# Halo rows of a fused attention and gated-FFN kernel: computed twice, or taken from the neighbouring token column

## The chip, the core and the metric

The kernel runs on one core of one Trainium2 chip. The metric is device time in microseconds (us) of one execution. Five engines matter: TensorE (PE, with its weight loads PEld), VectorE (DVE), ScalarE (ACT), GpSimd (POOL), and SyncE (SP), whose queue issues most of the transfers.

## The reference, cut to what matters

```python
# attention: x (4, 4160, 192), weight_gen (4, 4160, 8 heads, 7 taps)
w = np.exp(weight_gen - np.max(weight_gen, axis=-1, keepdims=True))
w = w / (np.sum(w, axis=-1, keepdims=True) + 1e-09)
x_pad = np.concatenate([np.zeros((B, 6, D)), x], axis=1)
x_unf = x_pad[:, np.arange(S)[:, None] + np.arange(7)[None, :], :]
x = np.einsum('bshk,bskhg->bshg', w, x_unf.reshape(B, S, 7, 8, 24)).reshape(B, S, D)
# gated FFN: w_in (192, 1024), conv_w (3, 1024), w_out (1024, 192)
h = np.maximum(x @ w_in, 0.0)
hp = np.concatenate([zeros(B, 1, 1024), h, zeros(B, 1, 1024)], axis=1)
conv_out = sum(conv_w[k] * hp[:, k:k + S, :] for k in range(3))
out = (h / (1.0 + np.exp(-conv_out))) @ w_out
```

Each output token needs seven tokens of x (itself and the six before it), and h of its own token, of the one before and of the one after.

## The kernel before

The 4 x 4160 tokens are cut into 128 segments of 130 tokens, one to a partition of the attention part; the 32 segments of one batch lie on neighbouring partitions. A **row** is one token of every segment: 128 tokens, 130 apart. Attention for a row works with the 128 tokens on the partitions. Its result is transposed on PE, and from there on a row is 128 **columns** of a matrix whose partitions are channels.

The convolution needs the row before the first and the row after the last, which are tokens of neighbouring segments. The kernel before computes them again: it loads the neighbours' x and weights (`load_x`, `load_w`), runs attention and the first matmul on row -1 and row 130 like on any other, and thus has 132 rows in 33 **blocks** of four (`R = 4`, `NB = 33`). Block 0 holds rows -1 to 2, block 32 rows 127 to 130. Rows outside a batch are zeroed with masks (`edge`, `zero`, `keep`).

Per block:

- **Attention** (`attention`, `head`, `tap`): seven products of x and the softmaxed weights ("taps") into the tiles px (taps 0 to 3) and py (taps 4 to 6). Weights come in **groups**: group 0 serves block 0, group 1 blocks 1 and 2, group 2 blocks 3 and 4. `SMX` names, by group, the engines of the softmax's subtraction and of its normalisation (with the zeroing). In blocks 0 to 2 PE transposes all seven taps and adds them up in a PSUM bank (two banks, tp for channels 0 to 127, ops for the other 64); `PLAN` names the engine of each tap. Later blocks add the taps by transfers.
- **Split** (`split_hi`, `split_lo`): the sum is split in two parts of lower precision, the tiles H1, H2 and L1.
- **Eight units**, one for 128 channels of h each (`unit`): five matmuls of 512 columns into a bank z (`mm1`); on ACT relu into h and the middle term of the convolution back into z (`relu`, `wmid`); on DVE the two side terms (`conv_side`, once per neighbour); on ACT the gate as a tanh (`sig`); on DVE the product into g (`gmul`). There are five banks z (`NZ = 5`), so a unit's first matmul waits for the `gmul` five units earlier.
- **Tiles** (`out_tiles`): for each row 8 pairs of matmuls of 192 columns, g times w_out, into a bank; ACT copies it out (`evac`), SP stores it (`store`). The tiles of a block stand on PE among the units of the block two later, except at the end; the tiles of block 1 stand among the units of block 2. Block j gives the rows whose neighbour after is known, so block 0 gives two rows, the others four.
- **Carry** (`carry`): the last two rows of h are copied to its front for the next block.

Before block 0 can finish, w_in, conv_w and w_out are decoded on ACT and DVE from their raw words (`dec`); `CH` lists the pieces of w_in, `WOE` names the engines for w_out, `FORD` the order of block 0's units.

The order on each engine isn't written out by hand. A list of tasks with estimated durations is put in order by a planner: earliest start first, then the rank `now` (block number plus an offset: `TO` for attention, `FO` for transposes, `WO_` for tiles), then one pass backward and one forward. All instructions are issued in this order, and every engine runs its own in order. Task kind "VK" marks DVE work that the planner keeps apart from POOL work: behind it DVE and POOL each write a one-column tile `tok`, and POOL waits there for DVE.

## Time and profile before

| | |
|---|---|
| three timed runs, median (range) | 707.25 us (706.74 to 707.96) |
| the profiled execution | 706.31 us |
| its span (first to last instruction) | 704.3 us |
| PE busy | 683.6 us, 97% |
| DVE busy | 629.0 us, 89% |
| ACT busy | 554.5 us, 79% |
| POOL busy | 514.9 us, 73% |
| granted TensorE clock | 0.999 |

The span is what the trace shows; the execution's own time has 2.0 us more around it. Busy shares are averages over stages. In rows of the timeline, the first two numbers are start and duration in us, and what stands in brackets is how long the engine had nothing to run before it, and what ended that.

### The profile page before, as it was taken

How to read it: one execution, taken by the hardware profiler on the slowest of the kernel's cores; microseconds unless marked ns; L12 is line 12 of the kernel's file. 1: busy time of each engine (PE TensorE's matmuls, PEld its weight loads, DVE VectorE, ACT ScalarE, POOL GpSimd, SP SyncE). 2: the span in 40 equal slices, each digit the busy share in tenths (PEclk: the TensorE clock that was granted, in tenths of full speed). 3: DMA queues.
4: the chain of work that ended last, by engine and by line, in shares of the span. 5: the costliest groups of instructions: out<-in, count | busy, mean ns of one | idle time of the engine just before them, and what ended most of it. 6: DMA issues, size and time to landing. Idle time of an engine off the chain costs nothing.

```text
span 704.3 us, 10972 instructions
## 1 busy us (share of the span) xinstructions
PE 683.6 (97%) x3749; PEld 623.3 (89%) x3749; DVE 629.0 (89%) x1005; ACT 554.5 (79%) x1079; POOL 514.9 (73%) x422
## 2 busy tenths in 40 slices
PE   1899999999999999999999999999999999999998
PEld 1788999999999999999999999999999999999998
DVE  6999999999999999999899899988898888888881
ACT  3588888887888888878787787888878778888881
POOL 3998987998999888897776878877777788730000
PEclk9999999999999999999999999999999999999999
DMA  7736998999999888797988889788888887781211
GB/s 236 214 92 166 218 205 207 211 226 213 207 223 217 202 199 194 178 207 170 218 190 201 197 163 223 176 213 193 189 188 184 177 184 167 171 194 67 78 44 45
DMA packets 70787, 127.59 MB, mean 181 GB/s; under 512 B 5046, under 2 KB 42573, under 8 KB 70732
## 3 DMA queue, kind: packets, MB, share of 16 engines
q0 software_dynamic: 20160, 58.99, 47.5%
q1 hardware_dynamic: 50090, 67.51, 29.6%
q8 instruction: 29, 0.48, 0.3%
q10 hardware_dynamic: 482, 0.40, 0.2%
q14 instruction: 26, 0.21, 0.1%
HBM read 20.51 MB, written 12.78 MB: 47 GB/s over the span
## 4 chain that ended last, share of the span: by engine, by line
PE 96%; DVE 2%; DMA 1%; POOL 0%; issue 0%; ACT 0%; POOLq 0%
PE ops L424 47%; PE z L378 43%; PE tp L340 4%; PE ops L340 1%; DMA stage<-in_moe_conv_w_dram 1%; PE z L424 1%; DMA stage<-in_moe_w_in_dram 0%; DVE py L292 0%; POOL px L292 0%; POOL py L292 0%; DVE r L257 0%; DVE m L248 0%; DVE w L242 0%; DVE px L292 0%; DVE dps L146 0%
## 5 line engine op out<-in xcount | busy, mean ns | idle before, releaser
L395 DVE SCALAR_TENSOR_TENSOR z<-h,cw,z 128x512 f32<-128x512 f32 (+1 forms) x528 | 377.6, 742 | 21.6 <-ACT z L388 15.7
L424 PE MATMUL ops<-wo,g 128*128 128x192 f32 x2048 | 353.1, 326 | 0.0
L424 PEld LDWEIGHTS ops<-wo,g 128*128 128x128 f32 x2048 | 338.9, 190 | 9.8
L378 PE MATMUL z<-H,wi 128*128 128x512 f32 x1056 | 303.8, 409 | 1.0 <-ACT wi L614 1.0
L292 POOL TENSOR_TENSOR px<-ring,w 128x768 f32<-128x768 f32 (+2 forms) x146 | 230.9, 1698 | 67.2 <-PE tp L340 67.0
L378 PEld LDWEIGHTS z<-H,wi 128*128 128x128 f32 x1056 | 191.1, 188 | 32.8 <-ACT wi L614 1.4
L402 ACT ACTIVATE z<-z 128x512 f32<-128x512 f32 (+1 forms) x264 | 150.7, 571 | 53.4 <-DVE z L395 51.7
L411 DVE SCALAR_TENSOR_TENSOR g<-z,h 128x512 f32<-128x512 f32 (+1 forms) x264 | 177.0, 678 | 12.3 <-ACT z L402 10.3
L388 ACT ACTIVATE z<-h,cw 128x512 f32<-128x512 f32 (+1 forms) x264 | 179.7, 684 | 6.2
L384 ACT ACTIVATE h<-z 128x512 f32<-128x512 f32 x264 | 155.4, 591 | 15.8 <-PE z L378 15.6
L292 POOL TENSOR_TENSOR py<-ring,w 128x768 f32<-128x768 f32 (+2 forms) x108 | 163.3, 1826 | 2.2 <-DMA px<-py 2.2
L378 PE MATMUL z<-L,wi 128*128 128x512 f32 x264 | 103.0, 390 | 0.0
L325 POOL TENSOR_TENSOR px<-px 128x512 f32<-128x512 f32 (+1 forms) x60 | 72.9, 1466 | 5.3 <-DMA px<-px 5.3
L360 ACT ACTIVATE H<-tp 64x256 fp32r<-64x256 f32 (+1 forms) x93 | 42.3, 454 | 22.0 <-PE tp L340 21.7
L378 PEld LDWEIGHTS z<-L,wi 128*128 128x128 f32 x264 | 49.5, 188 | 11.2
L433 ACT ACTIVATE o<-ops 128x192 f32<-128x192 f32 x128 | 42.1, 329 | 19.2 <-PE ops L424 16.7
L318 POOL DMA_DIRECT2D px<-px x30 | 36.7, 1224 | 15.3 <-DMA px<-py 12.9
L315 POOL DMA_DIRECT2D px<-py x30 | 40.4, 1346 | 8.5 <-POOL py L292 8.5
L340 PE MATMUL tp<-ident,px 128*128 128x128 f32 x228 | 38.0, 281 | 2.8 <-POOL px L292 2.0
L340 PEld LDWEIGHTS tp<-ident,px 128*128 128x128 f32 x228 | 30.0, 145 | 8.7 <-POOL px L292 2.5
L364 DVE TENSOR_TENSOR H<-tp,H 64x256 fp32r<-64x256 f32 x60 | 25.4, 423 | 7.7 <-ACT H L360 5.8
L364 DVE TENSOR_TENSOR L<-tp,H 128x512 fp32r<-128x512 f32 x33 | 22.7, 688 | 8.7 <-ACT H L360 8.6
(67 smaller groups left out, 181.4 us busy)
## 6 DMA issues: line engine op xcount, KB each, us to landing
px<-py POOLq DMA_DIRECT2D x30, 1152.0 KB, 9.9
h<-h SPq DMA_DIRECT2D x128, 256.0 KB, 4.4
px<-px POOLq DMA_DIRECT2D x30, 768.0 KB, 6.6
ring<-in_x_dram SPq DMA_DIRECT2D x31, 384.0 KB, 6.7
out_dram<-o SPq DMA_DIRECT2D x31, 384.0 KB, 5.8
w<-in_weight_gen_dram SPq DMA_DIRECT2D x15, 224.0 KB, 6.0
r_out<-in_moe_w_out_dram SPq DMA_DIRECT2D x4, 384.0 KB, 5.6
wi<-scr SPq DMA_DIRECT2D x8, 128.0 KB, 6.2
```

The costliest lines, as they stand in the source:

```text
L292: eng.tensor_tensor(out=dst[:, a:b, :].rearrange("p s (h g) -> p s h g", g=GRP), in0=ring[:, p:p + n, :].rearrange("p s (h g) -> p s h g", ...
L325: nc.gpsimd.tensor_tensor(out=dst.rearrange("p (s d) -> p s d", s=R), in0=a[:, :, lo:hi], in1=b[:, :, lo:hi], op=ALU.add)
L340: nc.tensor.matmul(o, lhsT=a, rhs=ident, is_transpose=True, start=(start and c == 0), stop=(stop and c == len(ops) - 1))
L360: nc.scalar.activation(out=hi, in_=src, func=ACTF.Copy)
L364: nc.vector.tensor_tensor(out=lo, in0=src, in1=hi.bitcast(F32), op=ALU.subtract)
L378: nc.tensor.matmul(out=z, lhsT=w[:, fs], rhs=h_t[j, nm], start=(i == 0), stop=(i == len(terms) - 1))
L384: nc.scalar.activation(out=hrow(f, 2, R), in_=z_t[j, f], func=ACTF.Relu)
L388: nc.scalar.activation(out=z_t[j, f][:, :no * P], in_=hrow(f, cc, no), func=ACTF.Copy, scale=cw[:, NF + f:NF + f + 1])
L395: nc.vector.scalar_tensor_tensor(out=z, in0=hrow(f, cc + d, no), scalar=cw[:, k * NF + f:k * NF + f + 1], in1=z, op0=ALU.mult, op1=ALU.add,)
L402: nc.scalar.activation(out=z, in_=z, func=ACTF.Tanh, scale=0.5)
L411: nc.vector.scalar_tensor_tensor(out=g_of(j, f), in0=z_t[j, f][:, :no * P], scalar=1.0, in1=hrow(f, cc, no), op0=ALU.add, op1=ALU.mult)
L424: nc.tensor.matmul(out=ps[:, 0:D], lhsT=g_of(j, f)[:, i * P:(i + 1) * P], rhs=wo[:, f, :], start=(f == 0), stop=(f == NF - 1),)
```

## The change

The halo rows are no longer computed. Block 0 has three rows (0 to 2), block 32 has three (127 to 129). A row that needs a neighbour's h takes it from the neighbouring column of the same matrix: row 130 of a segment is row 0 of the next, row -1 is row 129 of the one before.

- **Block 0**: x from six tokens back and not seven, no extra weight row, taps of 576 and not 768 elements, three transposes a tap, matmuls of 384 columns. Row 0's convolution is left open: `side_next` puts its middle and following terms in the SBUF tile `zs`, and only row 1 is finished. Row 2 is finished by block 1, as before. `keep0` copies h of row 0 to the tile `hs`, four transfers of two units each.
- **Block 32**: matmuls of 384 columns; row 129's following term comes from `hs`, shifted by one column inside a batch (128x4x31), so that the first side term takes two instructions.
- **Row 0's end**: when block 32's h is there, `left0` adds the missing term from row 129, one column to the left, eight times; `sig0` and `gmul0` work on four units at once; then row 0's tile (`row0`) is computed and stored.
- **Chosen anew**: softmax engines (group 0 "GV" for "VV", group 1 "GG" for "VV", group 3 "VV" for "GG"), the first piece of w_in decoded in SBUF with its clamp and remainder on POOL, the order of block 0's units, the ranks TO, FO, WO_, the assumed arrival times, and `WOE` (of whose letters only the last counts here).

```diff
-SMX = ("VV", "VV", "GG", "GG")
+SMX = ("GV", "GG", "GG", "VV")
-TO = -2.7
-FO = -0.35
-WO_ = 1.62
+TO = -1.55
+FO = -0.4
+WO_ = 1.52
-    ("f", 0, 256, 5.2, "VGP", "G"),
-    ("m", 0, 256, 8.7, "VVP", "G"),
+    ("f", 0, 256, 5.2, "GVS", "G"),
+    ("m", 0, 256, 10.4, "VVP", "G"),
-FORD = (0, 3, 1, 5, 2, 4, 7, 6)
+FORD = (0, 1, 3, 2, 7, 5, 4, 6)
...
+    def fresh(j):
+
+        return (0 if j else 1), (R if j < NB - 1 else R - 1)
...
+        a, b = fresh(j)
         for i, (w, nm) in enumerate(terms):
-            nc.tensor.matmul(out=z, lhsT=w[:, fs], rhs=h_t[j, nm], start=(i == 0), stop=(i == len(terms) - 1))
+            nc.tensor.matmul(out=z[:, a * P:b * P], lhsT=w[:, fs], rhs=h_t[j, nm][:, a * P:b * P], start=(i == 0), stop=(i == len(terms) - 1))
...
+    def side_next(j, f):
         no, cc = geom(j)
+        z = z_t[j, f]
+        if j == 0:
+
+            side(zs[:, f], hrow(f, cc + 1, 1), z[:, 0:P], 2, f)
+            side(z[:, P:2 * P], hrow(f, cc + 2, 1), z[:, P:2 * P], 2, f)
+        elif j == NB - 1:
+
+            n = (no - 1) * P
+            side(z[:, :n], hrow(f, cc + 1, no - 1), z[:, :n], 2, f)
+            zl_ = by_seq(z[:, n:n + P])[:, :, 0:PB - 1]
+            side(zl_, by_seq(hs[:, f])[:, :, 1:PB], zl_, 2, f)
...
+    def left0(f):
+        z = by_seq(zs[:, f])[:, :, 1:PB]
+        side(z, by_seq(h[:, f, R, :])[:, :, 0:PB - 1], z, 0, f)
...
+    def keep0(f0):
+        nc.sync.dma_start(out=hs[:, f0:f0 + CG, :], in_=h[:, f0:f0 + CG, 3, :])
...
         out_tiles(NB - 2)
+        now[0] = NB - 1 + WO_
+        hold0 = {}
+
+        def row0():
+            hold0[0] = mm2(NB, 0)
+        a_ = task("P", 0.03 + NF * 0.326, rd0 + bank[1], row0)
...
         out_tiles(NB - 1)
```

The order on the engines moves with it. Three places matter; in the rows the names are the tiles of the code with a running number, so px_305 and px_286 are block 1's px before and after, and each row ends with partitions x elements and a count.

**POOL, from block 0's py taps to block 1's first taps.** Before:

```order
L895 MEMSET tok2_101 128x1
L292 TENSOR_TENSOR py_218<-ring_98,w_118 128x768
L895 MEMSET tok3_102 128x1
L895 MEMSET tok4_103 128x1
L292 TENSOR_TENSOR px_185<-ring_98,w_118 128x768
L242 TENSOR_TENSOR w_143<-w_143,m_278 128x448
L292 TENSOR_TENSOR px_305<-ring_98,w_135 128x768 x2
```

After, where w_134 is group 1's weights and w_142 group 2's:

```order
L279 TENSOR_TENSOR px_174<-ring_98,w_120 128x576 x2
L227 TENSOR_TENSOR w_134<-w_134,m_187 128x448
L953 MEMSET tok2_101 128x1
L279 TENSOR_TENSOR py_208<-ring_98,w_120 128x576 x2
L245 TENSOR_TENSOR w_134<-w_134,r_188 128x448
L953 MEMSET tok3_102 128x1
L279 TENSOR_TENSOR px_174<-ring_98,w_120 128x576
L227 TENSOR_TENSOR w_142<-w_142,m_241 128x448
L251 TENSOR_TENSOR w_134<-w_134,edge_93 128x168
L279 TENSOR_TENSOR px_286<-ring_98,w_134 128x768 x3
```

Group 1's subtraction, normalisation and zeroing now stand on POOL among block 0's taps; there are two waits for DVE where there were three, and the two py taps stand behind one of them together.

**PE, from block 0's tiles to the first tile of block 1.** Before (g_403 is block 0's, g_649 block 1's; z_751 to z_794 are the first five units of block 2):

```order
L424 MATMUL ops_709<-wo_96,g_403 128x192 x8
L424 MATMUL ops_728<-wo_96,g_403 128x192 x8
L378 MATMUL z_751<-H1_680,wi_95 128x512 x2
...
L378 MATMUL z_794<-L1_681,wi_95 128x512
L424 MATMUL ops_804<-wo_96,g_649 128x192 x8
```

After (g_366 is block 0's, g_663 block 1's; z_677 to z_702 are the last three units of block 1, z_723 to z_778 the first five of block 2):

```order
L458 MATMUL ops_653<-wo_96,g_366 128x192 x8
...
L372 MATMUL z_677<-H1_456,wi_95 128x512 x2
...
L372 MATMUL z_702<-L1_457,wi_95 128x512
L372 MATMUL z_723<-H1_648,wi_95 128x512 x2
...
L372 MATMUL z_778<-L1_649,wi_95 128x512
L458 MATMUL ops_786<-wo_96,g_663 128x192 x8
```

One tile of block 0 is left there, and it has moved ahead of three units of block 1; nothing but units stands between it and block 1's first tile.

**DVE, the last unit of block 32.** Before (z_6211 and z_6237 are the last two units):

```order
L395 SCALAR_TENSOR_TENSOR z_6237<-h_97,cw_94,z_6237 128x512 x2
L411 SCALAR_TENSOR_TENSOR g_6172<-z_6211,h_97 128x512
L411 SCALAR_TENSOR_TENSOR g_6172<-z_6237,h_97 128x512
```

After (z_6197 and z_6223 are the last two):

```order
L388 SCALAR_TENSOR_TENSOR z_6223<-h_97,cw_94,z_6223 128x384
L388 SCALAR_TENSOR_TENSOR z_6223<-hs_109,cw_94,z_6223 128x4x31
L388 SCALAR_TENSOR_TENSOR z_6223<-h_97,cw_94,z_6223 128x512
L444 SCALAR_TENSOR_TENSOR g_6157<-z_6197,h_97 128x512
L444 SCALAR_TENSOR_TENSOR g_6157<-z_6223,h_97 128x512
L388 SCALAR_TENSOR_TENSOR zs_110<-h_97,cw_94,zs_110 128x4x31 x6
L425 SCALAR_TENSOR_TENSOR zs_110<-zs_110,hs_109 128x512 x2
```

Each unit has three side instructions and not two, and six of the eight `left0` and both `gmul0` come behind the last `gmul`; on PE row 0's tile follows directly on the first of block 32's four.

## Rows read from the trace of the kernel before

**Rows 1.** The page: span, and busy time, share and instructions by engine.

```profile
span 704.3 us, 10972 instructions
PE 683.6 (97%) x3749; PEld 623.3 (89%) x3749; DVE 629.0 (89%) x1005; ACT 554.5 (79%) x1079; POOL 514.9 (73%) x422
```

**Rows 2.** The chain that ended last, first 100 us: start, duration, what.

```profile
28.36 3.23 PE z L378 x13
...
64.18 5.68 PE z L378 x25
69.86 2.60 PE ops L424 x16
```

**Rows 3.** Timeline of PE at the start.

```profile
18.48 1.06 PE L340 MATMUL tp<-ident,px 128*128 128x128 f32 x4
19.34 1.06 PE L340 MATMUL ops<-ident,px 128*64 128x128 f32 x4
...
22.11 0.60 PE L340 MATMUL tp<-ident,py 128*128 128x128 f32 x4
22.54 0.60 PE L340 MATMUL ops<-ident,py 128*64 128x128 f32 x4
...
28.36 0.70 PE L378 MATMUL z<-H,wi 128*128 128x512 f32 x2 [1.01 <-ACT wi L614]
```

**Rows 4.** Timeline of DVE, the first 29 us.

```profile
5.00 0.39 DVE L239 TENSOR_REDUCE m<-w 128x32 f32<-128x224 f32 x1 [1.56 <-DMA w<-in_weight_gen_dram]
...
15.72 0.94 DVE L292 TENSOR_TENSOR px<-ring,w 128x768 f32<-128x768 f32 x1
...
17.99 1.70 DVE L292 TENSOR_TENSOR py<-ring,w 128x768 f32<-128x768 f32 x1
...
28.30 0.42 DVE L619 TENSOR_TENSOR wi<-dps,wi 128x256 fp32r<-128x256 f32 x1
```

**Rows 5.** Timeline of POOL, the first 25 us.

```profile
11.96 1.54 POOL L292 TENSOR_TENSOR px<-ring,w 128x768 f32<-128x768 f32 x1
...
17.34 1.54 POOL L292 TENSOR_TENSOR py<-ring,w 128x768 f32<-128x768 f32 x1
...
22.21 1.55 POOL L292 TENSOR_TENSOR px<-ring,w 128x768 f32<-128x768 f32 x1
23.71 0.97 POOL L242 TENSOR_TENSOR w<-w,m 128x448 f32<-128x448 f32 x1
```

**Rows 6.** DMA issues of the first 3 us, with us from issue to landing.

```profile
ring<-in_x_dram SPq DMA_DIRECT2D x1, 588.0 KB, 7.0
...
w<-in_weight_gen_dram ACTq DMA_DIRECT2D x1, 84.0 KB, 2.5
...
w<-in_weight_gen_dram ACTq DMA_DIRECT2D x1, 3.3 KB, 3.0
```

**Rows 7.** DVE groups by form, 28.6 to 67.5 us: busy us, mean ns.

```profile
L395 DVE SCALAR_TENSOR_TENSOR z<-h,cw,z 128x512 f32<-128x512 f32 x16 | 11.1, 745 | 0.0
L395 DVE SCALAR_TENSOR_TENSOR z<-h,cw,z 128x256 f32<-128x256 f32 x16 | 7.2, 476 | 0.0
...
L411 DVE SCALAR_TENSOR_TENSOR g<-z,h 128x256 f32<-128x256 f32 x8 | 3.3, 409 | 0.0
```

**Rows 8.** Timeline of DVE, the last two gmul of block 1.

```profile
66.11 1.35 DVE L411 SCALAR_TENSOR_TENSOR g<-z,h 128x512 f32<-128x512 f32 x2
```

**Rows 9.** The chain that ended last, its last 20 us.

```profile
685.58 5.20 PE ops L424 x32
690.78 2.60 PE z L424 x16
...
701.22 0.33 ACT o L433
```

**Rows 10.** Timeline of DVE, its last instructions.

```profile
688.42 1.43 DVE L411 SCALAR_TENSOR_TENSOR g<-z,h 128x512 f32<-128x512 f32 x2
```

**Rows 11.** Waits of DVE, 655 to 705 us: total us, times, longest.

```profile
DVE z L395 <- ACT z L388: 2.3, 4, 1.0
```

More of the change, by code (lines that the diff above doesn't have):

```diff
@@ L121 @@
     scr = [const.tile([P, 3, W], I32, name=f"scr{i}") for i in range(2)]
+    hs = const.tile([P, NF, P], F32, name="hs")
+    zs = const.tile([P, NF, P], F32, name="zs")
     EXP_OFF = 2.0 ** -112
@@ L279, in sm_ops, with cols @@
         )
+    def cols(q):
+        return (0 if q else 1), R
     def tap_cut(q, k):
@@ L286, in tap @@
         c = R - tap_cut(q, k)
-        for a, b in ((0, c), (c, R)):
-            if a == b:
+        for a, b in ((0 if q else 1, c), (c, R)):
+            b = min(b, cols(q)[1])
+            if a >= b:
                 continue
@@ L337, in transposes @@
             src = piece(q, i)
-            ops = [(dst[0:D2 if part else P, c * P:(c + 1) * P], src[:, c, part * P:part * D2 + P]) for c in range(R)]
+            ops = [(dst[0:D2 if part else P, c * P:(c + 1) * P], src[:, c, part * P:part * D2 + P])
+                   for c in range(cols(q)[0], R)]
         for c, (o, a) in enumerate(ops):
@@ L430, in evac @@
     def evac(j, i, ps):
-        if i == 0:
+        if j not in o_t:
             o_t[j] = o_p.tile([P, R, D], F32, tag="o", name="o")
@@ L713, in head @@
                     pr = i < 0 and part == 1
-                    f_ = task("P", 0.24 if pr else 0.46, [e_] + (bank[b_] if first else [prev[part]]), fold)
+                    f_ = task("P", 0.24 if pr else 0.46 if q else 0.35, [e_] + (bank[b_] if first else [prev[part]]), fold)
                     prev[part] = f_
@@ L724, in head, with tile_rows @@
                 yf_.append(task("none", 0.0, yend))
-        zl, last_mm, mm_end = [], [None], {}
+        zl, last_mm, mm_end, hk, l0, rd0 = [], [None], {}, {}, [], []
+        def tile_rows(j):
+            return range(0 if j else 1, geom(j)[0])
         def unit(j, f):
@@ L731, in unit @@
             now[0] = j + (FORD.index(f) if j == 0 else f) / NF
+            nr = fresh(j)[1] - fresh(j)[0]
             mm[n] = task(
[L733 removed]
+                "P", 1.135 if nr == R else 0.86, spl_done[j] + w_rdy[f] + zl[-NZ:][:1] * (len(zl) >= NZ),
+                lambda: mm1(j, f), after=[last_mm[0]])
             last_mm[0] = mm_end[j] = mm[n]
[L735 to L739 removed]
+            no = geom(j)[0]
+            m_ = (no if j else 1) * P
+            r_ = task("A", act(nr * P), [mm[n], ca.get(n - NF), hk.get(n - NF)] + ([] if j else [c2]), lambda: relu(j, f))
+            y_ = task("A", act(no * P, 1) + 0.04, [r_, c2], lambda: wmid(j, f))
+            cv_ = task("V", vec(m_) + 0.27 * (nr < R), [y_] + ([hk[f]] if j == NB - 1 else []), lambda: side_next(j, f))
+            cv_ = task("V", vec(m_), [cv_], lambda: side_prev(j, f))
             t_ = task("A", act(m_) + 0.02, [cv_], lambda: sig(j, f))
[L741 removed]
+            dep = [tiles[j - 2, i] for i in tile_rows(j - 2)] if j >= 2 else wo_rdy if j else []
             rd[n] = gm[n] = task("V", vec(m_, 0), [t_] + dep, lambda: gmul(j, f))
+            if j == NB - 1:
+                l0.append(task("VK", vec(P, 0), [r_], lambda: left0(f)))
+                if f % 4 == 3:
+                    a_ = task("A", act(W), l0[-4:], lambda: sig0(f - 3, f + 1))
+                    rd0.append(task("VK", vec(W, 0), [a_], lambda: gmul0(f - 3, f + 1)))
             zl.append(gm[n])
@@ L749, in unit @@
                     ca[k] = c_
+                if j == 0:
+                    c_ = dma(0.2 * CG, [gm[k] for k in ns], lambda: keep0(f0))
+                    for k in ns:
+                        hk[k] = c_
         zfree, last_evac, stored = [], [], []
@@ L754, in out_tiles @@
             d_ = 0.03 + NF * 0.326
-            no = geom(j)[0]
-            for i in range(no):
+            for i in tile_rows(j):
                 now[0] = j + WO_ + i / R
@@ L766, in out_tiles @@
                     after=[tiles.get((j, i - 1))])
[L767 removed]
+                e_ = task("A", act(D) + 0.02, [a_] + (stored[-4:][:1] if i == tile_rows(j)[0] and len(stored) > 3 else []),
                           lambda hold=hold: evac(*hold[0]), begun=last_evac)
@@ L793 @@
         out_tiles(NB - 2)
+        now[0] = NB - 1 + WO_
[3 more added lines that the diff above has]
+        a_ = task("P", 0.03 + NF * 0.326, rd0 + bank[1], row0)
+        e_ = task("A", act(D) + 0.02, [a_] + stored[-4:][:1], lambda: evac(*hold0[0]), begun=last_evac)
+        last_evac[:] = [e_]
+        bank[1] = [e_]
+        stored.append(dma(0.4, [e_], lambda: store(NB, 0, 1)))
         out_tiles(NB - 1)
```

100 lines of the change are left out of this document (45 added, 55 removed).

## The prediction

> **What bounds the kernel now.** I read the page first: PE is busy for 97% of a span of 704.3 us, DVE for 89% [rows 1]. The chain that ended last says the same more sharply. From 28.36 us to the end it runs on PE alone [rows 2]; the last piece is the copy of the last tile at 701.22 [rows 9]. Ahead of 28.36 PE waits for the first sums of taps, for their split and for the decoded w_in, and what is late there is made by POOL and DVE in turn. So the change can gain in three places: less work on PE, an earlier start of PE's unbroken run, and a shorter end. The timelines of DVE and POOL at the start, and of DVE where block 1 ends, say how much of each arrives at the last tile.
>
> **Less work on PE.** 25 matmuls of 512 columns take 5.68 us [rows 2], 0.227 each and 1.135 for a unit of five. No row has a matmul of 384 columns of this kind. In proportion it takes 0.170 and a unit saves 0.28; at worst it costs what 512 columns cost and saves nothing. I take 0.27, near proportion: 2.2 us for the eight units of block 0 and 2.2 for those of block 32, each between 0 and 2.3. Block 0 also has 14 transposes fewer, but they lie ahead of the unbroken run. The tiles stay 130 of 2.60 us; one of block 0's two moves to the end. That is nothing in PE's total, but 2.6 us of cover less at the start and 2.6 us of work more at the end.
>
> **The start on POOL.** Before, the first POOL tap begins at 11.96 and block 0's last tap at 22.21, so it ends at 23.7 [rows 5]. The weights of group 0 need one transfer and not three: the segments' own landed 2.5 us after issue, the last little one 3.0 after its later issue [rows 6], and DVE waited 1.56 us for it until 5.00 [rows 4]. That moves the softmax by about 1.4 us, but x then ends last: its 588 KB took 7.0 us to land [rows 6], and six rows in place of seven make that perhaps half a microsecond less, so x is there at about 9.6. Then come DVE's first tap (0.94 us for four rows [rows 4], 0.7 for three), two small decode steps and the hand-over: POOL's first tap at about 11.1, bounds 10.6 and 12.0. A tap of three rows is 1.54 x 3/4 = 1.16 us. Two taps end at 13.4; group 1's subtraction, moved here from DVE (0.97 us for its like on POOL [rows 5]), at 14.4; exponential, sum and hand-over take 1.2, to 15.6; two py taps to 18.0; the normalisation to 19.0. The third hand-over waits for DVE's decode of conv_w and of the next piece of w_in, 0.8; the last tap ends at 21.0, which is 2.7 us earlier than before.
>
> **From the last tap to the units.** Four transposes take 0.86 us start to start at 18.48 and 0.43 at 22.11 [rows 3]; the granted clock is 0.999 of 2.4 GHz over the execution and doesn't explain the two, so I price by these rates as they stand. PE stands mostly still until 19 us after the change, and 18 transposes of block 0 then follow the last hand-overs: 2.0 us at the fast rate, 3.9 at the slow one, and 1.1 for the split. The first unit starts at 24.1 to 26.0; I take 24.7. Before, the first unit had two of its five matmuls done and a wait of 1.01 us when the run began at 28.36 [rows 3], which is as if it had begun at 27.9. DVE's last step for the second piece of w_in ended at 28.7 [rows 4]; with the split ahead of it by 2.7 us less some idle time it ends at about 26.4, bounds 25.5 and 27.5.
>
> **DVE from there to the end of block 1.** Before, DVE goes from 28.7 to the last gmul of block 1, which ends at 67.4 [rows 8]: 38.7 us, almost without idle time. The list stays the same but for block 0's units. An instruction of 512 columns takes 0.745, of 256 columns 0.476 [rows 7], start to start 0.08 less; the straight line through these gives 0.26 for 128 columns (0.19 for a gmul, from its 0.409). A unit had two sides and a gmul of 256 columns, 1.11 us; it gets three sides and a gmul of 128, 0.97. Eight units save 1.1 us and the narrower splits 0.3, while one side of block 2, 0.66, now stands ahead of the last gmul: 38.0 us. That gmul then ends at 26.4 + 38.0 = 64.4, bounds 62.5 and 66.0.
>
> **What PE does meanwhile.** By PE's own work, block 1's first tile would come at 24.7 + 6.9 (block 0's units) + 12.1 (112 transposes at 0.108) + 9.1 (block 1's units) + 2.6 (a tile) + 5.7 (five units of block 2) = 61.1. But the fifth unit of block 2 needs the bank that the last gmul of block 1 gives back, and the tile needs its g. So that unit starts at 64.5 and the tile at 65.7: PE, which was the bound here, waits about 4.6 us for DVE over the first units of block 2. Before, the tile came at 69.86 [rows 2] and DVE had been ready 1 us ahead of the fifth unit. Shift: **-4.2 us**, between -6 and -2.5.
>
> **From that tile to the last.** PE's work is the same but for 2.2 us less in block 32 and row 0's tile, 2.6 more: **+0.4**. In the blocks between, PE is full and DVE is not; the softmax of group 3, moved to DVE, lies behind the shift and takes its idle time there. The saved rows' transfers and the eight new ones (h to hs) are off the path: block 1 reads h back only after its own units.
>
> **The end.** PE's last unit ends at 685.58, two tiles cover 5.20, and block 32's first tile begins at 690.78 [rows 9]; DVE's last gmul ends at 689.85 [rows 10], 0.9 earlier. After the change PE comes to this point 2.2 us sooner, while DVE has more to do: a unit's following term costs 0.26 for 31 x 4 columns more and 0.13 less for the 384, eight times 0.13, and two of the `left0` stand ahead of the last gmul, 0.5: 1.6 us. Together that is 3.7 against 0.9 of room and against the idle time that DVE has there, of which 2.3 us is waiting for ACT's middle term [rows 11]. Row 0's tile begins 2.6 after block 32's first and needs six `left0` and one `gmul0` behind the last gmul, 6 x 0.26 + 0.65 = 2.2. If no idle time is given up, PE waits 3.7 - 0.9 + 2.2 - 2.6 = 2.4 us; if all is, nothing. I take **+0.6**.
>
> **Sum.** -4.2 + 0.4 + 0.6 = -3.2 us. Against the profiled execution, 706.31 with 2.0 us around its span, that is 703.1. The median of the timed runs, 707.25, lies 0.94 above this execution, so the forecast for a median is 704.0. A change under 0.2%, 1.4 us, can't be told from none here.
>
> **Rivals.** (A) *DVE doesn't hold PE back.* If DVE gets through its list faster, with earlier inputs from PE, the tile comes when PE's own work allows, at 61.1: -8.8 + 0.4 + 0.6 = -7.8, 699.4. For it: PE is the only bound that the chain shows. Against it: DVE's 38.7 us for block 0 and 1 had no idle time to give, and half of A is the most that I'd expect. (B) *The end eats it.* DVE gives up no idle time and PE waits the 2.4 us: 705.8. For it: DVE's waits there are for ACT, which has a fixed order too. (C) *The hand-overs cost more than the narrower taps save: slower.* Place: DVE's instructions between the three `tok` waits. DVE's py tap took 1.70 us where its px tap took 0.94 [rows 4]; POOL's tap ran from 17.34 to 18.88 [rows 5], so it waited 0.8 for POOL. With group 1's softmax on POOL, three DVE steps (its py tap and two steps for conv_w) can each meet a POOL instruction of about 1 us, and POOL then waits at the next tok for what DVE did late. From a last tap at 24.2 on, 3.2 later than I have it, nothing is left; three full collisions and conv_w landing 1.5 late make 4.5, 708.5. The Trainium skill's page "SBUF — State Buffer", section "SBUF: two separate sides", says that DVE and GpSimd share a port pair as an exclusive lock, held for a whole instruction; the 0.8 us in this trace agrees. (D) *384 columns cost as much as 512*: the change doesn't do what it says on PE; block 32 saves nothing, +2.2: 706.2.
>
> **How the numbers follow.** Forecast 0.62, A 0.13, B 0.12, C 0.08, D 0.05. The time is the forecast's, 704.0; its own range by the bounds of DVE's front and of the end is 701.5 to 706. The range to hold 8 in 10 reaches down past A to 698.9 and up past B and D to 706.4. Faster by over 0.2% means below 705.8: the forecast but for 0.02 of it, A, and half of B, 0.79. Within 0.2%: the other half of B, D, and 0.03 of the forecast and of C, 0.14. Slower: the rest of C, 0.07.
>
> **What the profile after would show.** Right: a first unit on PE at 24 to 26 us with matmuls of 384 columns at about 0.175 start to start; DVE without idle time from 26 to 64; PE idle before z in the first units of block 2, released by DVE's gmul; block 1's first tile at about 65.7; a period of PE per block as before; at the end, waits of PE under 1 us around row 0's tile. Wrong: that tile at 61 with no wait (A); PE waiting over 2 us for zs (B); POOL's last tap of block 0 behind 23.7 (C); the units of block 32 still 1.135 apart (D).

## The result, and the profile after

The changed kernel takes **717.53 us**, median of four runs (714.57 to 719.27), against 707.41 for the kernel before (706.74 to 707.96): a ratio of 1.0139, with a 95% interval of 1.0104 to 1.0174. It is slower by 1.4%, outside the range of the prediction and on its other side. The profiled execution is the one of 717.59 us.

The page, answering to [rows 1]:

```profile
span 715.9 us, 10928 instructions
PE 685.7 (96%) x3735; PEld 624.3 (87%) x3735; DVE 630.9 (88%) x1026; ACT 562.0 (79%) x1081; POOL 514.2 (72%) x424
```

The span grew by 11.6 us while no engine has notably more to do: PE is 2.1 us busier with 14 matmuls fewer. The chain that ended last gives the first hint. Before, 96% of it ran on PE; now it does for 74%, with 8% on transfers and 8% on POOL. So somewhere PE now waits for a chain of POOL work and transfers. The timeline of PE shows where (start, duration, what; in brackets the idle time before it and what ended it):

```profile
26.90 0.96 PE L372 MATMUL z<-H,wi 128*128 128x384 f32 x4
...
27.88 0.85 PE L372 MATMUL z<-H,wi 128*128 128x384 f32 x4
...
28.75 0.60 PE L328 MATMUL tp<-ident,px 128*128 128x128 f32 x4
...
64.82 1.19 PE L372 MATMUL z<-H,wi 128*128 128x512 f32 x4 [1.15 <-DVE g L444]
...
68.69 2.76 PE L458 MATMUL ops<-wo,g 128*128 128x192 f32 x16
72.72 1.20 PE L372 MATMUL z<-H,wi 128*128 128x512 f32 x4 [1.27 <-DVE g L444]
...
90.92 2.76 PE L458 MATMUL ops<-wo,g 128*128 128x192 f32 x16
...
285.14 0.72 PE L372 MATMUL z<-H,wi 128*128 128x512 f32 x2 [2.11 <-ACT h L379]
...
286.09 4.25 PE L458 MATMUL ops<-wo,g 128*128 128x192 f32 x16
...
448.64 0.41 PE L328 MATMUL tp<-ident,px 128*128 128x128 f32 x2 [3.02 <-DVE L L353]
448.88 4.45 PE L458 MATMUL ops<-wo,g 128*128 128x192 f32 x16
...
702.11 2.76 PE L458 MATMUL ops<-wo,zs 128*128 128x192 f32 x16
```

In the timeline of before, the first tiles of blocks 1 and 2 are:

```profile
69.70 2.76 PE L424 MATMUL ops<-wo,g 128*128 128x192 f32 x16
...
89.91 2.76 PE L424 MATMUL ops<-wo,g 128*128 128x192 f32 x16
```

The reader is to see three things. Block 1's first tile stands at 68.69, where it stood at 69.70 (69.86 in the chain, [rows 2]). The start has thus gained 1.0 us, not 4.2. Of that nothing is left at block 2's first tile, 90.92 now and 89.91 before. In the middle of the program, where PE never stood still before, it stands still for 2.11 and 3.02 us, and the tile behind each stop takes 4.25 and 4.45 us instead of 2.76; a third, shorter stop, 0.83 us at 409.37, lies between them. And the end is as it should be: row 0's tile at 702.11 has no wait at all, where 0.6 was forecast. The last matmul ends at 712.7, 11.5 later than before.

The steady part can be told by one row of a table by stretch (window, its length, PE's busy time with its instructions, granted clock, share and rate of transfers), first before, then after:

```profile
125.00:660.00 535.00, 535.00 (x2909) 1.00 0.83 190
```

```profile
125.00:660.00 535.00, 529.04 (x2855) 0.99 0.83 188
...
286.00:288.00 2.00, 2.00 (x7) 0.50 0.01 0
...
450.00:453.00 3.00, 3.00 (x11) 0.51 0.33 99
```

Before, PE has no idle time in these 535 us. After, it has 5.96, and behind each of the two stops the granted clock is at 0.50 and 0.51, the lower level of 1.2 GHz, so that 1.49 and 1.69 us more go to the two tiles. Between the tiles just before and after the stops PE loses 4.06 (256 to 300 us) and 5.9 us (341 to 468 us, the short stop included) against the kernel before. The account: +1.0 at block 2's first tile, +10.0 in the stops, some +0.4 in the rest: 11.4 of the 11.5.

**What PE waits for.** From block 3 on the taps are added by transfers, and POOL's queue issues them. A block's first sum (`fold1`, px<-py, 1152 KB) is issued after its last py tap; the second (`fold2`, px<-px) needs the first to have landed, and waits on POOL's queue with everything of POOL behind it; then `fold3` adds the last two parts on POOL. Each block goes once around this ring of POOL work and a transfer. Here is POOL before and after, at about the same time:

```profile
341.16 1.55 POOL L292 TENSOR_TENSOR px<-ring,w 128x768 f32<-128x768 f32 x1 [4.00 <-PE tp L340]
342.95 1.22 POOL L318 DMA_DIRECT2D px<-px  x1 [0.25 <-issue]
343.73 3.52 POOL L292 TENSOR_TENSOR px<-ring,w 128x768 f32<-128x768 f32 x2
...
353.17 1.73 POOL L315 DMA_DIRECT2D px<-py  x1
```

```profile
343.61 1.22 POOL L305 DMA_DIRECT2D px<-px  x1 [3.93 <-DMA px<-py]
346.27 4.54 POOL L279 TENSOR_TENSOR px<-ring,w 128x768 f32<-128x768 f32 x3 [1.44 <-PE tp L328]
...
357.20 1.24 POOL L302 DMA_DIRECT2D px<-py  x1
...
370.50 1.22 POOL L305 DMA_DIRECT2D px<-px  x1 [3.55 <-DMA px<-py]
```

Before, one px tap of the next block stands ahead of `fold2` (L318). POOL waits 4.00 us with that tap for PE, which still reads the tile that the tap will overwrite, and when it is done the transfer has landed too: the slack of the ring is used up in a wait for PE, and PE is the bound. After, `fold2` (L305, at 343.61) stands ahead of all the taps, and POOL waits for the landing first. From block 6 on this is so in four blocks; in the others the new order shifts other work. The waits of POOL over the whole execution say the same (total us, times, longest):

```profile
POOL px L292 <- PE tp L340: 67.0, 19, 4.9
POOL px L318 <- DMA px<-py: 12.9, 7, 5.0
```

```profile
POOL px L305 <- DMA px<-py: 47.8, 16, 6.0
POOL px L279 <- PE tp L328: 42.3, 12, 4.9
```

Together that is 90.1 us where it was 79.9, and now more for the transfer than for PE. And in the chain of after, ahead of the second stop, transfers stand in place of matmuls (two of four rows):

```profile
357.20 12.77 DMA px<-py
...
378.09 11.18 DMA px<-py
```

For the comparison of runs I use two numbers, worked out from the 27 pairs of issues in POOL's timeline from 100 to 720 us. **A** is the mean time from the issue of a `fold2` to that of the next `fold1`: POOL's part of the ring, work and waits. **T** is the mean from a `fold1` to its `fold2` where POOL waited for the landing: the transfer's part. Such turns are few (6 before, 14 after, one or two in e10 and e11). On the mean a ring has room as long as A + T lies under PE's 20.24 us a block. Before, A is 7.93 and T 10.56, together 18.5; after, 8.58 and 10.80 (longest 13.3), together 19.4. What the expectations call W is POOL's work alone in its part of the ring, added up from the mean times of taps and sums: 7.31 before, 7.86 after.

**The link to PE.** PE doesn't wait for the sums themselves in these 535 us. What it waits for shows on ACT and POOL, first at the first stop (the timelines of after):

```profile
281.52 0.58 ACT L230 ACTIVATE w<-w 128x448 f32<-128x448 f32 x1 [4.61 <-POOL w L227]
```

```profile
279.57 2.85 POOL L227 TENSOR_TENSOR w<-w,m 128x448 f32<-128x448 f32 x2
```

A softmax's subtraction (L227) stands on POOL behind a `fold2` that waited 3.40 us for px<-py; ACT's exponential waits for it, and in order behind that stand relu and the middle term of the units, for which PE then waits (`<-ACT h` at 285.14). The second stop comes by the same link, over ACT's gate and DVE's `gmul` and split (`<-DVE L` at 448.64), and so does the short one at 409.37:

```profile
445.98 0.58 ACT L230 ACTIVATE w<-w 128x448 f32<-128x448 f32 x1 [3.74 <-POOL w L227]
```

ACT's waits for this subtraction, over the whole execution before and after (total us, times, longest):

```profile
ACT w L245 <- POOL w L242: 5.8, 4, 2.5
```

```profile
ACT w L230 <- POOL w L227: 15.8, 6, 4.6
```

### The profile page after: what moved, and what is told of

Read it like the earlier page. It is cut to its first block, busy times and chain, and to the rows that moved or that the text cites. A ratio compares the mean times of both kernels' runs of the same rounds, so it can differ in the third digit from the quotient of the medians.

```text
span 715.9 us, 10928 instructions
## 1 busy us (share of the span) xinstructions
PE 685.7 (96%) x3735; PEld 624.3 (87%) x3735; DVE 630.9 (88%) x1026; ACT 562.0 (79%) x1081; POOL 514.2 (72%) x424
## 4 chain that ended last, share of the span: by engine, by line
PE 74%; DMA 8%; POOL 8%; DVE 6%; ACT 2%; issue 1%; SPq 0%; DVEq 0%; POOLq 0%
PE ops L458 39%; PE z L372 31%; DMA px<-py 6%; POOL py L279 3%; PE tp L328 3%; POOL px L279 3%; DVE z L388 2%; DMA ring<-in_x_dram 1%; DVE g L444 1%; PE z L458 1%; POOL px L305 1%; POOL px L312 1%; ACT h L379 1%; DMA out_dram<-o 0%; ACT z L383 0%
## 5 line engine op out<-in xcount | busy, mean ns | idle before, releaser
L388 DVE SCALAR_TENSOR_TENSOR z<-h,cw,z 128x512 f32<-128x512 f32 (+2 forms) x528 | 375.3, 736 | 31.6 <-ACT z L383 27.3
L372 PE MATMUL z<-H,wi 128*128 128x512 f32 (+1 forms) x1056 | 299.0, 404 | 8.0 <-DVE g L444 3.8
L379 ACT ACTIVATE h<-z 128x512 f32<-128x512 f32 (+1 forms) x264 | 154.4, 585 | 46.1 <-PE z L372 43.6
L434 ACT ACTIVATE z<-z 128x512 f32<-128x512 f32 (+1 forms) x264 | 147.8, 565 | 34.8 <-DVE z L388 30.8
L372 PE MATMUL z<-L,wi 128*128 128x512 f32 (+1 forms) x264 | 102.3, 387 | 0.0
L312 POOL TENSOR_TENSOR px<-px 128x512 f32<-128x512 f32 (+1 forms) x60 | 71.4, 1413 | 5.4 <-DMA px<-px 5.4
L305 POOL DMA_DIRECT2D px<-px x30 | 37.3, 1244 | 48.3 <-DMA px<-py 47.8
L467 ACT ACTIVATE o<-ops 128x192 f32<-128x192 f32 x128 | 41.9, 327 | 19.4 <-PE ops L458 19.3
L349 ACT ACTIVATE H<-tp 64x256 fp32r<-64x256 f32 (+2 forms) x93 | 42.4, 456 | 3.8 <-PE tp L328 1.9
L353 DVE TENSOR_TENSOR L<-tp,H 128x512 fp32r<-128x512 f32 (+1 forms) x33 | 22.7, 687 | 3.2 <-ACT H L349 1.7
```

The costliest lines, as they stand in the source:

```text
L305: nc.gpsimd.dma_start(out=fl4(px_t[q][:, 0:2]), in_=fl4(px_t[q][:, 2:4]), accum_op=ALU.add, max_dma_last_dim=3072)
L312: nc.gpsimd.tensor_tensor(out=dst.rearrange("p (s d) -> p s d", s=R), in0=a[:, :, lo:hi], in1=b[:, :, lo:hi], op=ALU.add)
L353: nc.vector.tensor_tensor(out=lo, in0=src, in1=hi.bitcast(F32), op=ALU.subtract)
L372: nc.tensor.matmul(out=z[:, a * P:b * P], lhsT=w[:, fs], rhs=h_t[j, nm][:, a * P:b * P], start=(i == 0), stop=(i == len(terms) - 1))
L379: nc.scalar.activation(out=hrow(f, 2 + a, b - a), in_=z_t[j, f][:, a * P:b * P], func=ACTF.Relu)
L388: nc.vector.scalar_tensor_tensor(out=out, in0=in0, scalar=cw[:, k * NF + f:k * NF + f + 1], in1=in1, op0=ALU.mult, op1=ALU.add)
```

## The experiments

Four questions: what in the change costs the time (rows, or order); whether the ring is the cause; whether the order can be mended; and what the three rows alone are worth. Each kernel was timed beside the kernel before on the same chip; the ratio goes by that kernel's median there, 706.55 to 708.42. "Idle" is 535 less PE's busy time from 125 to 660 us.

| kernel | median us | ratio (95%) | A | T | idle |
|---|---|---|---|---|---|
| before | 707.41 | | 7.93 | 10.56 | 0 |
| after | 717.53 | 1.0139 (1.0104 to 1.0174) | 8.58 | 10.80 | 5.96 |
| e1 | 720.64 | 1.0195 (1.0179 to 1.0211) | 8.14 | 11.22 | 0 |
| e2 | 724.21 | 1.0258 (1.0212 to 1.0304) | 8.87 | 11.02 | 7.17 |
| e3 | 708.05 | 1.0015 (1.0005 to 1.0026) | 7.80 | 11.00 | 0 |
| e4 | 731.74 | 1.0347 (1.0327 to 1.0366) | 8.98 | 11.23 | 14.15 |
| e5 | 711.73 | 1.0065 (1.0040 to 1.0089) | 7.41 | 11.42 | 0.81 |
| e6 | 713.93 | 1.0099 (1.0078 to 1.0120) | 8.15 | 11.15 | 4.77 |
| e7 | 740.57 | 1.0463 (1.0416 to 1.0509) | 10.79 | 10.25 | 26.9 |
| e8 | 708.96 | 1.0022 (1.0001 to 1.0043) | 7.81 | 11.03 | 0 |
| e9 | 714.78 | 1.0106 (1.0080 to 1.0132) | 6.75 | 11.58 | 0 |
| e10 | 714.91 | 1.0109 (1.0087 to 1.0131) | 7.03 | 9.98 | 0 |
| e11 | 716.39 | 1.0129 (1.0107 to 1.0151) | 7.50 | 10.92 | 0 |
| e12 | 722.64 | 1.0213 (1.0180 to 1.0247) | 7.46 | 10.85 | 0 |
| **e13** | **704.90** | 0.9958 (0.9946 to 0.9970) | 7.94 | 10.66 | 0 |
| e14 | 725.29 | 1.0251 (1.0233 to 1.0270) | 8.45 | 10.85 | 4.13 |
| e15 | 713.35 | 1.0075 (1.0060 to 1.0090) | 8.04 | 11.08 | 4.87 |
| e16 | 718.17 | 1.0138 (1.0119 to 1.0156) | 8.59 | 10.61 | 8.0 |

Three of the sixteen times lie in the range expected by the theory that I held (e9, e13, e16), and e8, e10 and e15 lie in their rivals'. The other ten lie in neither, e3 by 0.05 us: the stops and the signs could be told better than the times.

One reading goes through all the runs. In the nine kernels with idle time, ACT's longest wait from 125 to 660 us for POOL's softmax subtraction is 3.5 to 13.2 us; in the nine without, it is 2.5 or less, and in e1, too, where A + T is 19.4, it is only 1.8. So the ring makes POOL late, and PE feels it through the softmax's exponential on ACT. No run moved the exponential alone, so this link is read from rows and not tested.

### Rows or numbers (e1, e2)

e1 is the kernel after with every number of before (`SMX`, the ranks, the decoding, `FORD`, `WOE`, the arrival times); e2 is the kernel before with every number of after. The planner makes its own order of each.

> Three-row blocks with every number of the kernel before (SMX, TO, FO, WO_, CH, FORD, WOE, arrival of conv_w). Theory N, the loss comes from the numbers: no stop in the loop, PE's period 20.24 us per block from block 2 to the end, POOL's waits for px<-py near the 12.9 us of before; time 703 to 706. Rival R, the loss comes from the three-row blocks and their transfers whatever the numbers: the 4 and 6 us stops in the loop are there again, 713 to 719.

> The kernel before (four-row blocks 0 and 32) with every number of the changed kernel. Theory N: stops in the loop as in the changed kernel, POOL's waits for px<-py over 30 us, time 710 to 720. Rival R: period 20.24 throughout, 705 to 709.

Both are slower than before. e2 has four rows and no transfer less, yet it shows the illness of after: 7.17 us of idle time, and POOL waits 84.3 us in 25 places for px<-py. So the numbers alone bring it about. Of e2's loss some 9 us lie at the start, ahead of block 1's first tile, and some 10 in the loop. e1 is a surprise. Its loop is clean, but the first turn of the ring fails; POOL, and PE right behind it:

```profile
88.67 1.54 POOL L279 TENSOR_TENSOR py<-ring,w 128x768 f32<-128x768 f32 x1 [8.94 <-DMA px<-py]
```

```profile
91.49 1.12 PE L328 MATMUL tp<-ident,px 128*128 128x128 f32 x4 [9.87 <-POOL px L312]
```

`fold2` was issued at 72.43, the next block's `fold1` at 73.18 and landed at 88.6, and a py tap that overwrites what that `fold1` reads was planned ahead of the `fold3` that PE needs. By these rows the ten us are one order of two instructions. "The three rows" and "the numbers" are therefore no separate causes: what counts is the order that the planner makes of both.

### Which number (e3, e4, e5)

```diff
# e3
-TO = -1.55
-FO = -0.4
-WO_ = 1.52
+TO = -2.7
+FO = -0.35
+WO_ = 1.62
# e4
-SMX = ("GV", "GG", "GG", "VV")
+SMX = ("VV", "VV", "GG", "GG")
# e5
-WO_ = 1.52
+WO_ = 1.62
```

> The changed kernel with TO, FO and WO_ of before, all else as changed. Theory N in its narrow form, the ranks set the order in which POOL gets taps and softmax and thus make the transfers px<-py late: the stops of 4.1 and 5.9 us in the loop go, 705 to 708. Rival S, the softmax engines (group 3 on DVE, groups 0 and 1 on POOL) start the loop badly and it never recovers: stops stay, 713 to 719.

> The changed kernel with SMX of before, all else as changed, the ranks too. Theory N (ranks): stops in the loop stay, 712 to 718. Rival S (softmax engines): stops go, and block 2's first tile comes 1 to 2 us sooner than the 91.08 us of the changed kernel: 704 to 708.

> The changed kernel with one number of before, WO_ = 1.62 (rank of the tiles). Call W the work that stands on POOL between the issue of fold2 of one block and the issue of fold1 of the next; by the durations of taps and sums in the traces it is 7.31 us on the mean of the loop before, 7.86 in the changed kernel, and 6.68 here. Theory L (loop): W and the transfer px<-py of 10 to 13 us follow each other in a ring, and where the ring is longer than PE's 20.24 us per block PE stops; here no stop after 110 us, POOL's waits for px<-py under 25 us, 705 to 709. Rival S (start): the lead that POOL lost in the first blocks is what makes the later stops, whatever the order in the loop; the stops stay, 713 to 719.

With the three ranks of before the loop has no idle time and the kernel is at 708.05; the rank of the tiles alone brings back 5.8 us of the 10.1. The softmax engines of before make it worse, with 14.15 us of idle time: the new engines of the softmax, as a whole, are not the culprit; with these ranks they helped. e3 still doesn't gain on before: its loop is clean and the loss lies at its start (PE waits 1.38 and 2.02 us at 83 and 95 us, for H and for `fold3`).

### The ring, touched alone (e6, e7)

e6 is the kernel after, with `fold2` put behind the first px tap of the next block from block 6 on; e7 is the kernel before with `fold2` ahead of all of them. Nothing else is moved. That is four `fold2` in e6 and 26 in e7, so e7 goes much further than the change did.

```diff
# e6 (e7: seq.index(t_) < seq.index(i), and insert at seq.index(t_))
+        for q, i in f2.items():
+            t_ = tap0.get(q + 1)
+            if q >= 6 and t_ is not None and seq.index(i) < seq.index(t_):
+                seq.remove(i)
+                seq.insert(seq.index(t_) + 1, i)
```

> The changed kernel with POOL's order edited by hand from block 6 on: fold2 of a block is issued behind the first px tap of the next one, as in the kernel before, never ahead of all three. Nothing else moves, W is 7.61 on the mean in place of 7.86. Theory L: most of the two stops (4.1 and 5.9 us) goes, 707 to 711. Rival S: the order in the loop doesn't matter, 715 to 719.

> The kernel before with POOL's order edited by hand the other way from block 6 on: fold2 of a block is issued ahead of all px taps of the next one. W rises from 7.31 to 10.2 us on the mean; with a transfer of 10 to 11 us the ring is 20.2 to 21.2 us for a block. Theory L: POOL waits for px<-py in nearly every block, over 80 us in all, and PE stops in the loop, 709 to 727. Rival S: the start is that of before, so 706 to 708.

e7 is the clearest run of the study: one kind of instruction moved on one queue makes the kernel before 4.6% slower, with 26.9 us of idle time in the loop:

```profile
POOL px L318 <- DMA px<-py: 128.4, 27, 6.7
```

```profile
125.00:660.00 535.00, 508.11 (x2722) 0.98 0.80 181
```

The 12.9 us in 7 waits have become 128.4 in 27. Its A + T is 21.0, and it is the only kernel over PE's 20.24. e6 moves the four back and brings back only 3.6 of the 10 us; its stop at 445 us stays, 3.48 long. The place of `fold2` can ruin the loop, but it is not all that ails the kernel after.

### Mending the order (e8 to e12)

e8 takes the ranks of before and sets the first turns right by hand (each `fold2` ahead of the next block's py taps, each `fold3` ahead of those of the block after it, block 3's right behind block 4's `fold1`). e9 tells the planner that `fold1` occupies the transfer engines for 8.5 us; e10 is e9 with the hand edits of e8, e11 has the ranks of before too. e12 has those ranks and hand edits, an occupancy of 7.5 and group 3's softmax on POOL.

```diff
# e8
+        for q in sorted(f2):
+            for i, r in ((f2[q], q + 1), (f3[q], q + 2)):
+                p_ = min((seq.index(t_) for t_ in pyt.get(r, [])), default=nt)
+                if p_ < seq.index(i):
...
+                    seq.insert(max(p_, low + 1), i)
...
# e9
-                a_ = dadd([prod[i] for i in (0, 1, 2, 4, 5, 6)], 6.5, lambda: fold1(q), 0.82)
+                a_ = dadd([prod[i] for i in (0, 1, 2, 4, 5, 6)], 8.5, lambda: fold1(q), 0.82)
```

> The changed kernel with the ranks of before and POOL's order mended by hand in the first folded blocks: no py tap stands ahead of the fold2 and the sum (fold3) that are ready sooner, and the sum of block 3 follows directly on fold1 of block 4, ahead of two waits for DVE. Theory L with the same cause at the start: PE's waits of 1.4 us (for H of block 3) and 2.0 us (for the sum of block 4) shrink or go, and the earlier start of the units shows for the first time, 703 to 706. Rival: PE waits there for the transfers themselves, which are late by the loads of x and weights; 707 to 709 as without the mending.

> The changed kernel with one estimate of the planner raised: a transfer px<-py counts 11.7 us in place of 9.7 (the traces show 10.3 to 11.4 on the mean where POOL waits for it, up to 13.7). W is 6.08 us on the mean in place of 7.86. Theory L: no stop in the loop after 110 us. But at the start the planner now puts fold2 of block 3 behind fold1 of block 4, so that its transfer stands behind one of 10 us in the queue; by the same theory PE then stops for 6 to 12 us before 100 us: 713 to 720 in all, with the loop clean. Rival S (the loop's stops come from the start): a stop at the start is followed by stops in the loop, over 720; or no stop at the start, and 706 to 709.

> As the run with the raised estimate, but with POOL's order mended by hand in the first folded blocks: fold2 of block 3 ahead of block 4's py taps, the sum of block 3 directly behind fold1 of block 4. Theory L: the stop at the start goes too and the loop is clean: 705 to 709, that is the changed kernel without its 10 us of stops in the loop. Rival S: 713 or more.

> As the run before, with the ranks TO, FO and WO_ of the kernel before as well. Loop clean; the start as in the runs with these ranks, where block 1's first tile came at 66.8 to 69.3 us: 704 to 709. If it beats the kernel before, the three-row blocks are worth something once POOL's order is right; if not, DVE, which is late by 2 us at block 3's split in those runs, holds the start.

> Ranks of before, POOL's order mended, the estimate at 10.7 us, and group 3's subtraction and normalisation back on POOL, where before they were. In the runs with them on DVE the subtraction took 2.7 to 2.8 us beside a POOL tap, in the first blocks where DVE has no idle time. Theory D (DVE holds the start): block 3's split comes 2 to 3 us sooner and the time is 702 to 706. Rival: POOL has no room for the two steps (1.9 us) and its folds are late: 707 to 711.

All five have a clean loop (A + T at most 18.8, idle 0), so the ring is mended, as expected. None is faster than before, where e8, e10, e11 and e12 were expected to come as low as 702 to 705. e8 is the best, at 1.0022. It is also the least steady, 705.45 to 711.37 over ten runs. The others lose 7 to 16 us around 100 us, each at a new spot. In e9 and e10 up to eight units stand in a row on PE, and there DVE, which needs longer for a unit than PE (two sides of 0.74 us and a `gmul` of 0.68, against 1.135), sets the pace. So e9's time is in its range by another way: PE was to stop there for a late sum, and its waits are for DVE. In e12 ACT and PE stand still together, PE for 8.52 us up to 103.22:

```profile
98.42 0.58 ACT L230 ACTIVATE w<-w 128x448 f32<-128x448 f32 x1 [9.04 <-POOL w L227]
```

The exponential waits 9 us for a subtraction on POOL, the same link as in the stops of after. These causes are read from rows; no run of their own tests them.

### Rows and order apart (e13, e14)

Since numbers can't separate the two, e13 keeps the three rows and issues the tasks in the very order of the kernel before, task by task, with that kernel's numbers. The few new tasks stand where their inputs are ready. e14 has four rows in the order of after.

```diff
-        for i in sorted(range(nt), key=lambda i: (best[i], pos[i])):
+        seq = [int(s_) for s_ in ORDER.split()]
...
+        for i in seq:
```

> Three-row blocks and every number of before, issued in the order of the kernel before, task by task (the planner's result is written into the kernel; the new tasks, keep0, left0, sig0, gmul0 and row 0's tile, stand where their inputs allow). Theory O (the order makes the loss, the three-row blocks don't): no stop in the loop, POOL's waits for px<-py as before; block 1's first tile up to 2.5 us earlier or no earlier, as DVE allows; 704.5 to 707.5. Rival R (the three-row blocks lose time by themselves): 709 or more.

> Four-row blocks with the changed kernel's numbers, issued in the order of the changed kernel, task by task (only block 0's two tiles stand some units later than its one tile there, since its second bank isn't free sooner). Theory O: the loss comes with the order: POOL's waits for px<-py over 35 us, stops in the loop, 712 to 722. Rival R: 705 to 709.

| | order of before | order of after |
|---|---|---|
| four rows | 707.5 | 725.3 |
| three rows | **704.9** | 717.5 |

The three rows are worth 2.6 us in the order of before. In the order of after they differ by 7.8, but that is no price of the rows: of the 17.8 us that this order costs four rows, 10.3 are there at block 2's first tile (100.20) and some 7 come in the loop, where after lost 1.0 and 10.0. The order costs the three rows 12.6. e13 is the fastest kernel here, at 704.77 to 704.95 in five runs, faster than before by 0.42% (0.30 to 0.54). Its timeline of PE:

```profile
64.16 1.20 PE L484 MATMUL z<-H,wi 128*128 128x512 f32 x4 [1.35 <-DVE g L556]
...
66.56 2.76 PE L570 MATMUL ops<-wo,g 128*128 128x192 f32 x16
...
689.30 2.87 PE L570 MATMUL ops<-wo,zs 128*128 128x192 f32 x16 [0.74 <-DVE zs L537]
```

Block 1's first tile comes 3.14 us earlier than before, PE waits for `gmul` ahead of the fourth unit of block 2, the loop has no idle time, and row 0's tile waits 0.74 us.

### One engine's order (e15, e16)

e15 is the kernel after with POOL's tasks from block 6 on in the sequence that they have in the kernel before, PE's and DVE's rows unchanged; e16 is the inverse, the kernel before with the sequence of after on POOL.

> The changed kernel; from block 6 on POOL's instructions stand in the order of the kernel before. The rows of PE and DVE don't change, those of SP and ACT in two and one places (a load of x, one exponential). W falls from 7.86 to 7.39 us. Theory L (POOL's order in the loop makes the two stops): no stop after 120 us, 707 to 710. Rival: the orders of PE, DVE and ACT make it too, 713 or more.

> The reverse: the kernel before, with POOL's instructions in the order of the changed kernel from block 6 on; PE's rows don't change. W rises from 7.31 to 7.86 us. Theory L: POOL's waits for px<-py over 30 us and stops of PE in the loop, 711 to 722. Rival: 706 to 709.

e16 loses 9.8 us against the kernel before beside it, with 8.0 of idle time, and shows the link over ACT again:

```profile
285.01 0.58 ACT L356 ACTIVATE w<-w 128x448 f32<-128x448 f32 x1 [8.26 <-POOL w L353]
```

```profile
290.69 0.66 PE L451 MATMUL tp<-ident,px 128*128 128x128 f32 x2 [7.29 <-DVE L L475]
```

The edit doesn't touch POOL alone: an exponential can't stand ahead of its subtraction, so two of ACT's moved along, and the one at 285.01, which ran at 261.93 in before, is one of them. That POOL's order alone is enough to cause such a loss is shown by e7, in which nothing moved on the other engines. e15 missed its expectation: it should have come to 707 to 710, and with 713.35 it brought back only 4.2 us. PE still stops at 158 and 446 us, for 2.24 and 2.62 us. Ahead of both, ACT waits for POOL's subtraction, 3.54 and 3.35 us. The stop at 446 is the second one of after; the one at 158 is new, and its exponential is the only one that moved:

```profile
148.15 0.58 ACT L342 ACTIVATE w<-w 128x448 f32<-128x448 f32 x1 [3.54 <-POOL w L339]
```

The order of ACT in after was made to match POOL's, and one sequence put back doesn't restore the other; that is a reading of these rows, and no run tests it.

## Why the prediction was wrong

**The start** (−4.2 forecast). The mechanism was right: PE waits for DVE's `gmul` over the first units of block 2, 2.5 us in three waits ahead of the tile (4.6 forecast); the size was not, −1.0 in after. The rows that answer to [rows 4 to 6], from the timelines of DVE and POOL and the transfers' issues:

```profile
26.88 0.56 DVE L353 TENSOR_TENSOR L<-tp,H 128x384 fp32r<-128x384 f32 x1 [1.66 <-ACT H L349]
...
28.23 0.42 DVE L653 TENSOR_TENSOR wi<-dps,wi 128x256 fp32r<-128x256 f32 x1
...
66.68 0.69 DVE L444 SCALAR_TENSOR_TENSOR g<-z,h 128x512 f32<-128x512 f32 x1
...
69.26 2.79 DVE L227 TENSOR_TENSOR w<-w,m 128x448 f32<-128x448 f32 x1
```

```profile
12.13 2.36 POOL L279 TENSOR_TENSOR px<-ring,w 128x576 f32<-128x576 f32 x2
...
20.82 1.20 POOL L279 TENSOR_TENSOR px<-ring,w 128x576 f32<-128x576 f32 x1
```

```profile
ring<-in_x_dram SPq DMA_DIRECT2D x1, 504.0 KB, 7.6
```

x is smaller and landed later, 7.6 us after issue instead of 7.0 [rows 6], so that everything from the first tap on is 1 us late: POOL's first tap at 12.13 (11.1 forecast), its last ends at 22.0 (21.0). The mis-sized term is the way from there to the units: PE did 24 transposes in a row from 20.94 to 26.11, all at the slow one of the two rates, where 18 had been priced between the two, so that the first unit came at 26.9 (24.7). DVE's split waited for them, 1.66 us up to 26.88. Its last step for the second piece of w_in stands behind the split and ended at 28.65 (26.4), which is as late as before, and the last `gmul` of block 1 at 67.37 (64.4). The prediction said that the granted clock doesn't explain the two rates, since it reads 0.999; that was a wrong reading, as the last section shows. In e13 the transposes go at the fast rate from about 19 us on, these two steps end at 25.93 and 64.76, and the term is −3.14. That is near the forecast, but in part by luck, since e13 has the engines and numbers of before and the prediction priced those of after.

**384 columns** were right: the five matmuls of a unit take 0.87 us, start to start (27.88 to the next instruction at 28.75); 0.865 was forecast.

**From that tile to the last** (+0.4 forecast). This is the step that failed, in its sentence "In the blocks between, PE is full and DVE is not; the softmax of group 3, moved to DVE, lies behind the shift and takes its idle time there." Its second half fails at once: group 3's subtraction takes 2.79 us on DVE at 69.26, among the `gmul`s and not in idle time, and PE waits 1.27 us for DVE at 72.72, most of the 2.0 us that it loses from there to block 2's first tile. For the rest I priced the loop by PE's and DVE's work and by nothing else. The ring of POOL and a transfer, 18.5 of 20.24 us long, I didn't price at all, though POOL's two kinds of wait in the trace of before (67.0 us for PE, 12.9 for px<-py) were there to be read. And I took a new order of the planner, which the ranks change in every block, for a change at both ends. In its place: A + T went to 19.4, POOL's subtraction came late for ACT's exponential, and the stops cost 10.0 us, 5.96 of it idle PE and 3.2 the half clock behind them. Over all runs, those with A + T up to 18.9 have at most 0.8 us of idle time, those from 19.1 on 4 to 27, not in strict order; one exception is e1, with 19.4 and none. The border lies under the 20.24 that the theory names: a mean over 27 turns says that the room is small, not which turn fails.

**The end** (+0.6 forecast): no wait in after, where DVE had time enough, 0.74 in e13.

**The rivals.** None was this one. A didn't happen: the tile didn't come at 61. B and D are refuted by the rows above. C ended on the right side, but at another place; POOL's last tap of block 0 ended at 22.0, ahead of 23.7.

Shown: that the order and not the rows costs the time (e13, e14), that POOL's sequence is enough to make such stops (e7), that the ranks bring them about (e3). Open: whether another place of the softmax's exponential on ACT would end the stops that e6 and e15 left, and why after's runs spread over 4.7 us where e13's stay within 0.2. That the stops hang on when a transfer lands, and that they reach PE by the exponential alone, is read from rows and not tested.

## What to carry to other kernels

Where an in-order queue both does work and waits for its own transfers, add up one turn of that ring (work, issue, landing) and hold it against the period of the engine that bounds the kernel; a wait for the bounding engine inside the ring is its slack, and an edit that turns it into a wait for the transfer is a loss in the making. Then look at what else waits for that queue: here the stops came where another in-order engine stood still 3.5 us or more for one short instruction on it. When a change makes a planner order everything anew, test the change in the old order first, task by task: here a gain of 0.4% lay under a loss of 1.8%.

## What the hardware showed that I had not expected

- After PE had stood still for 2.11 and 3.02 us, the granted clock of the next stretch was 0.50 and 0.51 of 2.4 GHz, and a tile took 4.25 and 4.45 us instead of 2.76. A stop can cost more than its length. Not each does: after e5's stop of 2.04 us at 81.24 and e2's of 2.15 at 418.81 the granted clock stayed at 1.00 (stretches of 83 to 86 and of 418 to 421 us).
- A granted clock of 1.00 can be a missing record. The trace of after has none of the clock ahead of 26.27 us, before none ahead of 20.52 and e13 none ahead of 18.92, and for such stretches the view prints 1.00. Nine transposes ahead of 26.27 take 0.213 us each, start to start, and four behind it 0.11 each:

```profile
23.55 2.13 PE L328 MATMUL tp<-ident,py 128*128 128x128 f32 x9
```

  In before and in e13, too, the spacing falls from 0.21 to between 0.11 and 0.13 where the records begin, with a granted clock of 1.00; up to then PE had done nothing but transposes in both. By these rows the two rates are the two levels, 1.2 and 2.4 GHz. The level ahead of the records is inferred and not read.

- An accumulating transfer of 1152 KB within SBUF took 11.2 and 12.8 us in the two rows of the chain above; the transfer engines were 83% busy on the mean of 125 to 660 us. The Trainium skill, "SBUF — State Buffer", section "The DMA setup-cost knee (why "@ 1 MiB" ≠ asymptote)", fits a transfer as 2 us plus its bytes over 436 GB/s. By that page the estimate would be 4.7 us; the measurement decides, and no run here shows the transfer alone.
- DVE's subtraction of 128x448 took 2.79 us at 69.26, beside a POOL tap that ran from 69.57 to 71.56; a multiplication of the same shape at 76.07, with POOL idle, took 0.61. The Trainium skill's "SBUF — State Buffer", section "SBUF: two separate sides", says that DVE and GpSimd lock each other out of a shared port pair for whole instructions. These rows agree in that the one ended 0.5 us behind the other, at 72.05; that the first to start gets the pair, as the page has it, they don't show, since DVE's record starts 0.3 us ahead of POOL's.
